# Attention-value products for two token tiles at once (256 columns) in two of six groups, with three wider transposed buffers and five staging buffers instead of seven

## The chip, the cores and the metric

One core of a Trainium2 chip runs the whole program. The metric is the device time of one execution in microseconds (us), the median over runs. The engines of the core run their own instruction streams in order: PE (TensorE: matmuls and transposes; PEld are its weight loads), DVE (VectorE), ACT (ScalarE), POOL (GpSimd) and SP, which here only starts DMA transfers.

## What is computed

```python
def _attn_ref(q, k, v):                      # 2 batches, 8 heads, 576 tokens, head size 64, fp32
    scores = scale * q @ k^T                 # per batch and head
    keep the 32 largest scores of each row, softmax over them
    return attn @ v

x = attention output as [1152 tokens, 512]
h = x @ w_in;  g = max(h, 0) + alpha * min(h, 0);  x = g @ w_out          # 512 -> 2048 -> 512
a = x @ w_a;   b = x @ w_b;                        out = (a * b) @ w_out2  # 512 -> 1536 -> 512
```

The weights arrive as 64-bit floats and are converted to fp32 on the chip.

## The kernel before, in words

**Token groups.** The 1152 tokens are cut into six groups (`M1`, line 46). A unit `('T', b, t)` is tile `t` of 128 tokens of batch `b`, `('L', b, 0)` the last 64 tokens of a batch. Groups 0, 1 and 5 hold one T tile, groups 2 and 4 two T tiles of one batch, group 3 two L units and a T tile. Attention walks the groups in order, in a group the four head pairs `hp`, and in a head pair the units. Each T unit gives two attention tiles, one for each head of the pair, each L unit one (lines 373 to 378): 72 attention tiles in all.

**One attention tile.** `front` (396) multiplies q with k into PSUM and ACT copies the 128x576 scores to `s`. `middle` (409) is the top-32 search on DVE (four MAX8, three MATCH_REPLACE8), the exponential on ACT, and the masked sum on DVE; POOL scales the rows (430). `back` (436) transposes the 576 columns in five pieces on PE (441, 443) and ACT copies them into a buffer `pt` of 5 x 128 columns (442, 444). `pt` has two buffers (`PB`, 41), one for each head of a pair. `back` of a tile is issued while DVE is in the next tile's search.

**The product with v.** When both heads of a unit are done, `av` (450) issues ten fp32 matmuls: for each of the five 128-row pieces one matmul for each head, with a 128x64 slice of `v` as the weights and `pt[:, c, :]` (128 columns) as the moving data. Head 0 writes the upper 64 partitions of the PSUM tile `o`, head 1 the lower 64. The profile records each fp32 matmul as two, so one call of `av` is 20 records and 20 weight loads, all at line 463. ACT (468) and DVE (469) then write `o` as two fp16 parts into `xT` of the group at the unit's columns (group 0 uses one ACT copy, line 471). `o` shares two PSUM buffers (tag "T") with the transposes of `back` and of `finish`. There are 40 calls of `av`: the 1st to 4th in time belong to group 0, the 5th to 8th to group 1, the next 8 to group 2, the next 12 to group 3, the next 8 to group 4, the last 4 to group 5.

**The two feed-forward stages.** For each group `moe1` (549) and `moe2` (636) run; `ORDER` (48) puts them in the order (1,0), (2,0), (1,1), (2,1), (1,2), (2,2), (1,3), (2,3), (1,4), (1,5), (2,4), (2,5), where the first number is the stage and the second the group. Matmuls into the hidden layers are at lines 530 and 534, those out of them at 542 and 545. The first chunk of `moe1`'s contraction over features is head pair 0, the last is head pair 3. The first stages use fp32 weights; later ones use weights split into two fp16 parts (`pair`, 239, on ACT and POOL), which for the last weight are kept in DRAM and fetched through three buffers `w2s` (`W2B`, 33).

**The staging ring.** Each of 68 weight blocks is loaded as 64-bit numbers into a staging buffer `raw` of 4 KB per partition (185) and read by ACT twice (190, 191) and by DVE once (192); POOL adds the parts (193). `RAWB` (53) is the number of such buffers, seven. Four tiles `v_raw` of `x_scale` (143) use the same ring; ACT squares them (141). The first 14 blocks are mixed with the first 8 attention tiles, then come the `v_raw` tiles, then 54 blocks, then the other attention tiles (line 52). When the last staging buffer is free, its space becomes that of the "late" pool (317), which holds `xT`, so that no group but group 0 can write `xT` earlier.

**Order.** The program is a single list of instructions with priorities; at build time each engine's order is fixed with the help of a simulated timeline (882), which also decides when a buffer is waited for. A different number of buffers or a different call can therefore change the order on every engine.

Of the kernel before, what the change touches and what calls it, by code (L numbers as in the profile page):

```python
# [8 lines left out]
F32 = mybir.dt.float32  # L9
# [7 lines left out]
AF = mybir.ActivationFunctionType  # L17
ALU = mybir.AluOpType

P = 128  # L20
B, H, S, D = 2, 8, 576, 64
# [16 lines left out]
OB = 2  # L38
EB = 3
WKB = 1  # L40
PB = 2
JB = 1
XB = 3
GB = 4
# [5 lines left out]
NATIVE = {(1, 0): (0, 0), (2, 0): (0, 0), (1, 1): (1, 0), (2, 1): (0, 0)}  # L50
STAGES = [(k, g if isinstance(g, tuple) else (g,)) + NATIVE.get((k, g), (1, 1)) for k, g in ORDER]
DVE = [('open', 0), ('mix', 14, 8), ('xs', 0), ('conv', 54), ('att', 80)]
RAWB = 7
FA = 4
QA = 1
VA = 0
# [24 lines left out]
def tile_topk_attention_moe(ctx: ExitStack, tc: tile.TileContext, qT, kT, vM, vL, wi, wo, al, wa, wb, w2, out):  # L81
    nc = tc.nc
    cp = ctx.enter_context(tc.tile_pool(name="cp", bufs=1))
    sp = ctx.enter_context(tc.tile_pool(name="sp", bufs=2))
# [4 lines left out]
    def psum(name, tag="H"):  # L89
        return pp.tile([P, 512], F32, tag=tag, name=name, bufs=2)  # L90
# [52 lines left out]
    def x_scale():  # L143
        for hp in range(4):
            v = early.tile([P, DM], I64, tag="raw", name="v_raw", bufs=RAWB).bitcast(F32)[:, 0:5 * P]
            v = v.rearrange("p (c n) -> p c n", c=5)
# [36 lines left out]
    def to_f32(dst, name, i):  # L183
        raw = early.tile([P, DM], I64, tag="raw", name="raw", bufs=RAWB)
        nc.sync.dma_start(raw, srcs[name][i])
        lo = raw.bitcast(U32).rearrange("p (n t) -> p n t", t=2)[:, :, 0]
        hi = raw.bitcast(I32).rearrange("p (n t) -> p n t", t=2)[:, :, 1]
        d = dst.bitcast(I32)
        r = early.tile([P, DM], I32, tag="rlo", name="rlo", bufs=RLOB)
        nc.scalar.activation(r.bitcast(I16).rearrange("p (n t) -> p n t", t=2)[:, :, 0], lo, AF.Copy, scale=2.0 ** -29)  # L190
        nc.scalar.activation(r.bitcast(BF16).rearrange("p (n t) -> p n t", t=2)[:, :, 1], hi.bitcast(F32), AF.Sign)
        nc.vector.tensor_scalar(d, hi, 3, None, op0=ALU.logical_shift_left)
        nc.gpsimd.tensor_tensor(out=d, in0=d, in1=r, op=ALU.add)
# [171 lines left out]
    tiles = []  # L365
    gsize = []
    for g, grp in enumerate(M1):
        cols_of = {}
        col = 0
        for kind, b, t in grp:  # L370
            cols_of[kind, b, t] = col
            col += P if kind == "T" else D
        for hp in range(4):
            for kind, b, t in grp:
                n = P if kind == "T" else D
                heads = [[2 * hp], [2 * hp + 1]] if kind == "T" else [[2 * hp, 2 * hp + 1]]
                for i, hs in enumerate(heads):
                    tiles.append(dict(g=g, b=b, t=t if kind == "T" else 4, hp=hp, hs=hs, n=n, col=cols_of[kind, b, t], last=i == len(heads) - 1))
        gsize.append(col)

    def fetch(tl):
# [53 lines left out]

    def back(tl):
        e = tl["e"]
        pt = sp.tile([P, 5, P], F32, tag="pt", name="pt", bufs=PB)
        t1, t2 = psum("t1", "T"), psum("t2", "T")
        for c in range(4):  # L440
            nc.tensor.transpose(t1[:, c * P:(c + 1) * P], e[:, c * P:(c + 1) * P], ident)  # L441
        nc.scalar.activation(pt[:, 0:4, :].rearrange("p c n -> p (c n)"), t1, AF.Copy)  # L442
        nc.tensor.transpose(t2[:, 0:P], e[:, S - P:S], ident)
        nc.scalar.activation(pt[:, 4, :], t2[:, 0:P], AF.Copy)
        tl["pt"] = pt

    def split_view(t):
        return t.rearrange("p c n -> p (c n)").bitcast(F16).rearrange("p (a c n) -> p a c n", a=2, c=4)

    def av(pair_):  # L450
        tl = pair_[-1]
        g, hp, n, col = tl["g"], tl["hp"], tl["n"], tl["col"]
        v = vcur[g, tl["b"], hp]
        if g not in xts:
            if split_in[g] or gsize[g] > P:
                xts[g] = late[0].tile([P, 4, 256], F32, tag="xT", name=f"xT{g}", bufs=XB)
            else:
                xts[g] = sp.tile([P, 4, P], F32, tag="xe", name=f"xe{g}", bufs=2)
        o = psum("o", "T")
        for c in range(5):  # L460
            for j in range(2):
                pt = pair_[j]["pt"] if n == P else tl["pt"]
                nc.tensor.matmul(o[j * D:(j + 1) * D, 0:P], v[:, c, j * D:(j + 1) * D], pt[:, c, :], start=c == 0, stop=c == 4)  # L463
        for r, c in [(slice(0, P), slice(0, P))] if n == P else [(slice(0, D), slice(0, D)), (slice(D, P), slice(D, P))]:
            if split_in[g]:
                x = split_view(xts[g])
                xh = x[r, 0, hp, col:col + n]
                nc.scalar.activation(xh, o[r, c], AF.Copy, scale=vsc[r, 0:1])
                nc.vector.scalar_tensor_tensor(x[r, 1, hp, col:col + n], o[r, c], vsc[r, 0:1], xh, op0=ALU.mult, op1=ALU.subtract)  # L469
            else:  # L470
                nc.scalar.activation(xts[g][r, hp, col:col + n], o[r, c], AF.Copy)

    def attention():
# [11 lines left out]
        for i, tl in enumerate(tiles):  # L485
            s = ready.pop(0)
            for k, _ in enumerate(middle(tl, s)):
                if k == 0 and i + FA < len(tiles):
                    fetch(tiles[i + FA])
                if k == 1 and i + VA < len(tiles):  # L490
                    fetch_v(tiles[i + VA])
                if k == KBACK and prev is not None:
                    back(prev)
                    pr.append(prev)
                    if prev["last"]:
                        av(pr)
                        pr = []
                    yield ("done", prev["g"])
                if k == KFRONT and i + QA < len(tiles):
                    ready.append(front(tiles[i + QA]))  # L500
                yield 1
            prev = tl
        back(prev)
        pr.append(prev)
        av(pr)
        yield ("done", prev["g"])

# [378 lines left out]
```

## Time and profile before

| what | value |
|---|---|
| median of three runs | 750.46 us (750.15 to 750.53) |
| the profiled execution, its own time | 752.66 us |
| its span, first to last instruction | 750.6 us |
| mean granted TensorE clock | 0.951 |
| instructions | 14910 |

The profiled execution is 2.2 us above the median, and 2.1 us of it lie outside the span. Busy times are sums over an engine's instructions; because matmul ends are modelled, a PE busy share of 100% says that PE never stood idle, not that it computed at its peak.

### The profile page before, as it was taken

Reading aid. Unit: us, or ns where it says so; the run is one execution under the profiler, and the core shown is the slowest. Engines: PE = TensorE matmul, PEld = TensorE weight load, DVE = VectorE, ACT = ScalarE, POOL = GpSimd, SP = SyncE. Lnnn points to the kernel's source line nnn. Section 1 sums busy time; section 2 is a strip of 40 time slices with the busy share of each in tenths; the row PEclk is TensorE's granted clock in tenths of the full one; section 3 lists DMA queues with packets and bytes.
Section 4 is the critical chain, followed back from the end, with each engine's and each line's share of the span. In section 5 each row is a group of like instructions: output and inputs, shape, how many; then the busy total and the mean of one; then the engine's idle time right before and its main releaser. Section 6 shows DMA issues by size and latency. Waiting matters only on the chain.

```text
span 750.6 us, 14910 instructions
## 1 busy us (share of the span) xinstructions
PE 653.1 (87%) x5162; PEld 491.0 (65%) x5162; DVE 600.7 (80%) x1478; ACT 476.8 (64%) x1011; POOL 394.2 (53%) x540
## 2 busy tenths in 40 slices
PE   2565677899979798989976999999899999999997
PEld 1354555587766586867745777776677777677775
DVE  3999999979799989899889968999899799222121
ACT  4869786977588677888887634555644455453222
POOL 5865888868465467878777522443233333131111
PEclk9997679899999898999998999999799999999999
DMA  6957977975420012330145632210122220001243
GB/s 198 332 142 257 312 255 257 320 275 195 136 71 24 11 59 70 94 90 22 55 129 177 185 90 67 77 28 12 30 66 65 73 74 1 2 1 43 72 127 99
DMA packets 60410, 86.16 MB, mean 115 GB/s; under 512 B 7984, under 2 KB 34608, under 8 KB 60336
## 3 DMA queue, kind: packets, MB, share of 16 engines
q1 hardware_dynamic: 59024, 82.87, 35.1%
q10 hardware_dynamic: 1312, 2.36, 0.9%
q8 instruction: 40, 0.66, 0.4%
q14 instruction: 34, 0.28, 0.1%
HBM read 76.55 MB, written 8.65 MB: 114 GB/s over the span
## 4 chain that ended last, share of the span: by engine, by line
PE 57%; DVE 21%; DMA 7%; ACT 7%; issue 4%; POOL 3%; SPq 1%; POOLq 0%; ACTq 0%; DVEq 0%
PE h L530 8%; PE y L542 7%; PE o L542 7%; PE ha L530 7%; PE hb L530 7%; PE o L463 5%; DVE wk L420 4%; DVE m L422 4%; DMA w2s<-w_st 3%; DVE e L426 3%; PE t L441 3%; PE ps L403 3%; PE ha L534 2%; PE hb L534 2%; PE o L545 2%
## 5 line engine op out<-in xcount | busy, mean ns | idle before, releaser
L422 DVE MAX8 m<-wk 128x8 f32<-128x576 f32 x216 | 162.9, 754 | 2.5
L521 POOL TENSOR_TENSOR gp<-gt,gp 128x256 f16<-128x256 f32 (+1 forms) x112 | 68.3, 611 | 153.9 <-ACT gp L520 143.8
L420 DVE MATCH_REPLACE8 wk<-m,wk 128x576 f32<-128x576 f32 x144 | 106.7, 741 | 0.0
L530 PE MATMUL h<-xT,wi_sb 128*128 128x256 f16 (+1 forms) x960 | 100.0, 253 | 2.3 <-DVE xT L469 1.3
L530 PEld LDWEIGHTS <-wi_sb 128*128 128x128 f16 x960 | 79.6, 99 | 22.9 <-issue 7.1
L430 POOL TENSOR_SCALAR e<-e,sm 128x576 f32<-128x576 f32 x72 | 55.1, 765 | 66.5 <-DVE sm L428 52.0
L542 PE MATMUL y<-wo_sb,gp 128*128 128x512 f16 x336 | 85.4, 380 | 1.7 <-ACT gp L520 1.7
L542 PEld LDWEIGHTS <-gp 128*128 128x128 f16 x588 | 54.7, 98 | 46.9 <-ACT gp L520 2.8
L520 ACT ACTIVATE gp<-gt 128x256 f16<-128x256 f32 (+1 forms) x112 | 43.2, 388 | 61.9 <-DVE gt L666 43.2
L426 DVE SCALAR_TENSOR_TENSOR e<-s,m,e 128x576 f32<-128x576 f32 x72 | 73.4, 1020 | 10.0 <-ACT e L416 7.7
L403 PE MATMUL ps<-ks,qh 128*128 128x288 f32 x160 | 49.4, 391 | 28.0 <-ACT s L406 15.2
L666 DVE SCALAR_TENSOR_TENSOR gt<-hb,wb_inv,r 128x256 f32<-128x256 f32 (+1 forms) x48 | 21.4, 446 | 61.6 <-PE hb L530 61.2
L463 PE MATMUL o<-pt,v 128*64 128x128 f32 x800 | 64.1, 298 | 6.3 <-ACT pt L442 3.8
L530 PE MATMUL ha<-xT,wa_sb 128*128 128x256 f16 (+1 forms) x576 | 66.0, 265 | 0.4 <-ACT xT L612 0.4
L414 DVE MAX8 m<-s 128x8 f32<-128x576 f32 x72 | 53.9, 748 | 15.2 <-ACT s L406 15.0
L542 PE MATMUL o<-w2s,gp 128*128 128x512 f16 x252 | 63.9, 379 | 1.8 <-DMA w2s<-w_pr 1.4
L463 PEld LDWEIGHTS o<-pt,v 128*64 128x64 f32 x800 | 49.3, 147 | 24.6 <-issue 7.8
L530 PE MATMUL hb<-xT,wb_sb 128*128 128x256 f16 (+1 forms) x576 | 65.2, 263 | 0.0
L416 ACT ACTIVATE e<-s,nb 128x576 f32<-128x576 f32 x72 | 55.7, 775 | 12.5 <-POOL nb L415 12.3
L530 PEld LDWEIGHTS <-wa_sb 128*128 128x128 f16 x576 | 51.7, 100 | 14.0 <-issue 2.1
L441 PE MATMUL t<-ident,e 128*128 128x128 f32 x288 | 50.5, 299 | 9.7 <-POOL e L430 4.4
L406 ACT ACTIVATE s<-ps 128x576 f32<-128x576 f32 x72 | 46.5, 645 | 17.9 <-DVE e L426 12.1
(191 smaller groups left out, 1455.0 us busy)
## 6 DMA issues: line engine op xcount, KB each, us to landing
w2s<-w_pr SPq DMA_DIRECT2D x48, 256.0 KB, 2.6
w2s<-w_st SPq DMA_DIRECT2D x36, 256.0 KB, 2.7
raw<-in_wi_dram SPq DMA_DIRECT2D x16, 512.0 KB, 5.8
raw<-in_wo_dram SPq DMA_DIRECT2D x16, 512.0 KB, 5.2
v<-in_vM_dram SPq DMA_DIRECT2D x28, 256.0 KB, 3.1
raw<-in_wa_dram SPq DMA_DIRECT2D x12, 512.0 KB, 4.5
raw<-in_wb_dram SPq DMA_DIRECT2D x12, 512.0 KB, 5.3
raw<-in_w_dram SPq DMA_DIRECT2D x12, 512.0 KB, 5.0
```

The lines of the kernel that those rows point to most:

```text
L403: nc.tensor.matmul(ps[:, f, 0:HALF], q[:, h % 2, :], ks[h][:, f * HALF:(f + 1) * HALF], start=i == 0, stop=i == len(mm) - 1)
L414: nc.vector.max(m8[:, 0:8], s)
L416: nc.scalar.activation(e, s, AF.Exp, bias=nb, scale=0.125)
L420: nc.vector.match_replace(out=wk, in_to_replace=m8[:, 8 * r - 8:8 * r], in_values=src, imm_value=NEG)
L422: nc.vector.max(m8[:, 8 * r:8 * r + 8], wk)
L426: nc.vector.scalar_tensor_tensor(e, s, m8[:, 31:32], e, op0=ALU.is_ge, op1=ALU.mult, accum_out=sm[:, 0:1])
L430: nc.gpsimd.tensor_scalar(e, e, sm[:, 1:2], 1.0, op0=ALU.mult, op1=ALU.mult)
L441: nc.tensor.transpose(t1[:, c * P:(c + 1) * P], e[:, c * P:(c + 1) * P], ident)
L463: nc.tensor.matmul(o[j * D:(j + 1) * D, 0:P], v[:, c, j * D:(j + 1) * D], pt[:, c, :], start=c == 0, stop=c == 4)
L521: nc.gpsimd.tensor_sub(l[:, 0:n], t[:, 0:n], h[:, 0:n])
L530: nc.tensor.matmul(dst[:, 0:n], w[a][:, c * P:(c + 1) * P], x[:, b, c, 0:n], start=k == 0, stop=k == 11)
L542: nc.tensor.matmul(dst, act[b][:, s], w[a], start=i == 0 and k == 0, stop=i == last and k == 2)
```

## The change

In groups 2 and 4 the two T units of a head pair become one unit of two slots. `back` writes each tile's transposed pieces into its 128 columns of a `pt` buffer that is now 5 x 256 columns wide in every group. `av` is called once for both slots, after the fourth attention tile instead of after the second and the fourth: ten matmuls with 256 columns instead of twice ten with 128, and then one ACT and one DVE instruction over 256 columns instead of two each over 128. The other groups keep 128 columns. `PB` goes from 2 to 3: `pt` takes 15 KB per partition instead of 5. `RAWB` goes from 7 to 5: the staging ring takes 20 KB per partition instead of 28.

```diff
-PB = 2
+PB = 3
-RAWB = 7
+RAWB = 5
...
+            units = []
             for kind, b, t in grp:
...
+                if units and len(units[-1]) < 2 and kind == "T" and units[-1][0][:2] == (kind, b):
+                    units[-1].append((kind, b, t))
+                else:
+                    units.append([(kind, b, t)])
+            for unit in units:
+                pts_of = {}
+                for slot, (kind, b, t) in enumerate(unit):
+                    n = P if kind == "T" else D
+                    heads = [[2 * hp], [2 * hp + 1]] if kind == "T" else [[2 * hp, 2 * hp + 1]]
+                    for i, hs in enumerate(heads):
+                        tiles.append(dict(g=g, b=b, t=t if kind == "T" else 4, hp=hp, hs=hs, n=n, col=cols_of[unit[0]], slot=slot,
+                                          wide=len(unit) * P, pts=pts_of, last=slot == len(unit) - 1 and i == len(heads) - 1))
...
     def back(tl):
...
-        pt = sp.tile([P, 5, P], F32, tag="pt", name="pt", bufs=PB)
+        j = tl["hs"][0] % 2
+        if tl["slot"] == 0:
+            tl["pts"][j] = sp.tile([P, 5, 2 * P], F32, tag="pt", name="pt", bufs=PB)
+        pt = tl["pts"][j][:, :, tl["slot"] * P:tl["slot"] * P + P]
...
     def av(pair_):
...
+        wd = tl["wide"]
         for c in range(5):
             for j in range(2):
-                pt = pair_[j]["pt"] if n == P else tl["pt"]
-                nc.tensor.matmul(o[j * D:(j + 1) * D, 0:P], v[:, c, j * D:(j + 1) * D], pt[:, c, :], start=c == 0, stop=c == 4)
-        for r, c in [(slice(0, P), slice(0, P))] if n == P else [(slice(0, D), slice(0, D)), (slice(D, P), slice(D, P))]:
+                pt = tl["pts"][j if n == P else 0]
+                nc.tensor.matmul(o[j * D:(j + 1) * D, 0:wd], v[:, c, j * D:(j + 1) * D], pt[:, c, 0:wd], start=c == 0, stop=c == 4)
+        if n == P:
+            n = wd
+        for r, c in [(slice(0, P), slice(0, wd))] if n > D else [(slice(0, D), slice(0, D)), (slice(D, P), slice(D, P))]:
```

## Rows read from the trace of the kernel before

**Rows 1.** The page's first part: busy time of each engine over the span, its share and its instructions.

```profile
PE 653.1 (87%) x5162; PEld 491.0 (65%) x5162; DVE 600.7 (80%) x1478; ACT 476.8 (64%) x1011; POOL 394.2 (53%) x540
```

**Rows 2.** The table by stretch: start and end in us, length, then busy us of PE, PEld, DVE, ACT and POOL (with instructions), granted clock, DMA share, GB/s. The stretches run from the first of the 54 blocks (61) to the opening of the late pool (192), on to the last call of group 2 (324), and then from the start of stage (2,2) (424) to that of stage (1,4) (598), to the end of attention (646) and to the end.

```profile
61.00:192.00 131.00, 103.81 (x705) 79.98 (x706) 122.36 (x310) 103.14 (x212) 103.73 (x109) 0.86 0.79 269
192.00:324.00 132.00, 118.11 (x901) 90.88 (x899) 121.21 (x325) 102.43 (x215) 82.12 (x107) 0.94 0.21 64
...
424.00:598.00 174.00, 170.47 (x1362) 127.92 (x1362) 155.56 (x371) 87.76 (x196) 56.08 (x100) 0.97 0.21 62
598.00:646.00 48.00, 48.00 (x393) 35.23 (x391) 37.96 (x89) 24.11 (x56) 16.20 (x27) 1.00 0.12 35
646.00:751.00 105.00, 99.47 (x977) 74.05 (x974) 22.52 (x62) 36.03 (x94) 20.64 (x41) 0.99 0.21 61
```

**Rows 3.** The chain of waits in order of time (start us, us on the chain, what): the fetches of the last split weight, the first matmuls of stage (2,2), and a call of `av` in group 4.

```profile
417.68 2.65 DMA w2s<-w_st
421.11 2.87 DMA w2s<-w_pr
424.02 1.46 PE o L542 x6
...
426.89 1.31 PE hb L530 x12
...
474.82 1.24 PE o L463 x20
```

**Rows 4.** The view of the tile `pt`: duration ns min/median/max, first and last start in us, forms; its weight loads.

```profile
L463 PEld LDWEIGHTS o<-pt,v x800: 132/137/232, 37.4 to 644.6; 128*64 128x64 f32 x160
```

**Rows 5.** PE's timeline (start us, us, engine, line, operation, count, idle time before it): calls of `av` in groups 2 (two) and 3, the last piece of the last call in group 4, and the first matmuls of stage (1,4).

```profile
297.95 2.40 PE L463 MATMUL o<-pt,v 128*64 128x128 f32 x20
...
324.17 1.31 PE L463 MATMUL o<-pt,v 128*64 128x128 f32 x20
...
415.51 1.09 PE L463 MATMUL o<-pt,v 128*64 128x128 f32 x16 [0.31 <-ACT pt L442]
...
585.83 0.43 PE L463 MATMUL o<-pt,v 128*64 128x128 f32 x2
...
597.63 0.71 PE L530 MATMUL h<-xT,wi_sb 128*128 128x256 f16 x5
```

**Rows 6.** Groups of ACT and DVE instructions by line and shape (count, busy us, mean ns of one, idle time before and its releaser): the reads of `o` at 128 columns, reads of other PSUM tiles at 256, and copies of 128x512 into a packed and into a strided tile.

```profile
L468 ACT ACTIVATE xT<-o,vsc 128x128 f16<-128x128 f32 x28 | 10.1, 364 | 13.3 <-PE o L463 13.2
L565 ACT ACTIVATE r<-h,pre_sig 128x256 f32<-128x256 f32 x48 | 22.5, 470 | 22.4 <-PE h L530 22.3
L469 DVE SCALAR_TENSOR_TENSOR xT<-o,vsc,xT 128x128 f16<-128x128 f32 x28 | 9.4, 339 | 2.3 <-ACT xT L468 2.2
L566 DVE SCALAR_TENSOR_TENSOR gt<-h,pre_alp,r 128x256 f32<-128x256 f32 x48 | 22.7, 474 | 7.7 <-ACT r L565 7.5
L619 ACT ACTIVATE xT<-tp 128x512 f32<-128x512 f32 x1 | 0.6, 597 | 0.0
L619 ACT ACTIVATE xe<-tp 128x512 f32<-128x512 f32 x1 | 0.6, 582 | 0.0
```

**Rows 7.** The timeline of DVE and PE after the last call of group 2.

```profile
326.27 2.76 DVE L426 SCALAR_TENSOR_TENSOR e<-s,m,e 128x576 f32<-128x576 f32 x1
...
329.69 0.34 DVE L469 SCALAR_TENSOR_TENSOR xT<-o,vsc,xT 128x128 f16<-128x128 f32 x1
...
331.11 0.61 PE L530 MATMUL h<-xT,wi_sb 128*128 128x256 f16 x4
```

**Rows 8.** Who waited for whom (us in total, times, longest): POOL on the last matmul of `av`, from 424 to 646 us.

```profile
POOL v L338 <- PE o L463: 8.6, 7, 2.9
```

**Rows 9.** The view of the tile `raw`: last blocks' loads and reads (first and last start), and the time from issue to landing of all its loads.

```profile
L185 SPq DMA_DIRECT2D raw<-in_w_dram x12: 327/328/358, 98.0 to 172.2; - x12
L192 DVE TENSOR_SCALAR wa_sb<-raw x12: 411/841/1495, 104.8 to 174.8; 128x512 int32<-128x512 int32 x12
L192 DVE TENSOR_SCALAR w2s<-raw x12: 411/488/1494, 109.1 to 191.5; 128x512 int32<-128x512 int32 x12
DMA to landing us min/median/max: 3.4/5.1/9.9
```

**Rows 10.** The timeline of SP, ACT and DVE where the 54 blocks begin: the ACT reads that free staging buffers, the first load of the 54, its DVE read, and ACT's first read of a `v_raw` tile.

```profile
60.17 0.75 ACT L191 ACTIVATE rlo<-raw 128x512 bf16<-128x512 f32 x1
60.95 0.34 SPq L185 DMA_DIRECT2D raw<-in_wi_dram  x1
62.66 0.76 ACT L191 ACTIVATE rlo<-raw 128x512 bf16<-128x512 f32 x1
64.39 1.39 DVE L192 TENSOR_SCALAR wi_sb<-raw 128x512 int32<-128x512 int32 x1 [0.17 <-DMA raw<-in_wi_dram]
64.47 0.73 ACT L141 ACTIVATE vsq<-v_raw 128x640 bf16<-128x640 f32 x1
```

**Rows 11.** SP's timeline where the third weight begins: three staging loads in a row.

```profile
92.08 0.52 SPq L185 DMA_DIRECT2D raw<-in_wa_dram  x1
...
96.12 0.33 SPq L185 DMA_DIRECT2D raw<-in_wb_dram  x1
98.04 0.33 SPq L185 DMA_DIRECT2D raw<-in_w_dram  x1
```

**Rows 12.** What SP's queue waited for (us in total, times, longest): staging loads on the ACT read that frees their buffer.

```profile
SPq L185 <- ACT rlo L191: 39.4, 29, 3.4
```

More of the change, by code (lines that the diff above doesn't have):

```diff
@@ L373, in tile_topk_attention_moe @@
         for hp in range(4):
+            units = []
             for kind, b, t in grp:
[L375 to L378, printed above, removed]
+                if units and len(units[-1]) < 2 and kind == "T" and units[-1][0][:2] == (kind, b):
[10 more added lines that the diff above has]
+                                          wide=len(unit) * P, pts=pts_of, last=slot == len(unit) - 1 and i == len(heads) - 1))
         gsize.append(col)
@@ L441, in back @@
             nc.tensor.transpose(t1[:, c * P:(c + 1) * P], e[:, c * P:(c + 1) * P], ident)
-        nc.scalar.activation(pt[:, 0:4, :].rearrange("p c n -> p (c n)"), t1, AF.Copy)
+        nc.scalar.activation(pt[:, 0:4, :], t1.rearrange("p (c n) -> p c n", c=4), AF.Copy)
         nc.tensor.transpose(t2[:, 0:P], e[:, S - P:S], ident)
         nc.scalar.activation(pt[:, 4, :], t2[:, 0:P], AF.Copy)
-        tl["pt"] = pt
     def split_view(t):
```

## The prediction, made before the changed kernel was run

> **What bounds the kernel now.** I read the busy shares first, then the table by stretch, then the chain of waits in time. The shares alone name PE: 653.1 of 750.6 us, with DVE at 600.7 [rows 1]. The stretches say where that is a limit. From 424 to 598 us PE is busy 170.47 of 174, then 48.00 of 48, then 99.47 of 105: 318 of the last 327 us, while DVE has 28 us to spare before attention ends at 646 and 82 of 105 after it [rows 2]. From there on the end is the sum of PE's work. Before it PE is idle: 27 us of the 131 from 61 to 192, 14 of the 132 to 324; there DVE, at 122.36 and 121.21, is nearer to its limit [rows 2]. PE's full stretch begins when the last split weight comes back from DRAM: the chain hops from fetch to fetch and enters stage (2,2) at 424 [rows 3]. So a PE microsecond saved behind 424 counts in full, one saved before it counts only if DVE or the conversion chain also moves.
>
> **The matmuls.** A call of av stands on the chain with 1.24 us for 20 records [rows 3]. How much of it is columns? A call of 20 records reads 1.31 us in the timeline, a piece of 16 reads 1.09 [rows 5], so a record costs (1.31 - 1.09) / 4 = 0.055 us. Twelve fp16 matmuls of 256 columns take 1.31 us, 0.109 each [rows 3], hence 0.055 for 128 columns. An fp32 record is two passes and the two heads fill two halves of the array at once; two passes over two halves is one pass, and 0.055 fits that. The 20 records are then 1.10 us of columns and 0.14 is the price of entering and leaving the half-array form. At 256 columns I expect 20 x 0.109 + 0.14 = 2.32 against 2 x 1.24 = 2.48: **0.16 us saved in each of 8 calls**. Four of them lie in group 4, between 474.82 [rows 3] and 585.83 [rows 5], where PE is full: -0.64. The four of group 2, 0.64 too, and more where the clock is low (one call there took 2.40 [rows 5]), lie where PE has 14 us idle; I count half, -0.3. The bounds of this term are 0 (columns alone, and all of group 2 hidden in idle time) and the rival below in which the loads set the pace.
>
> A rule speaks for more. The Trainium skill, "TensorE: Matmul & The Clock Gate", section "Back-to-back issue gap", gives a spacing per matmul of about 81 ns at 128 columns and 131 ns at 512, so four times the columns would cost 1.6 times; by it, as an estimate, a wide call would cost some 1.5 us and eight calls would save about 8 us. The trace speaks against it for this chain, where 256 columns cost twice the 0.055.
>
> **The reads of o.** In each of the eight pairs two ACT copies of 364 ns become one; the nearest row at 256 columns is 470 [rows 6]: -0.26 us, and I count nothing for it, since ACT is idle for a third of the span [rows 1]; the bound is group 2's four, -1.0. On DVE two of 339 become one near 474: -0.20 [rows 6]. For group 4 both are covered, since PE sets the time there; for group 2 DVE is 92% busy, so its 4 x 0.20 = 0.8 may count: bounds 0 and -0.8, I take -0.4. The shared PSUM pair "T" is asked for 8 times less; no row prices that alone, so it stays inside the bounds.
>
> **Writes to pt.** All 72 tiles now write a strided buffer. The one strided 128x512 copy took 597 ns, the packed one 582 [rows 6]: 72 x 0.015 = 1.1 us of ACT, spread over a span in which ACT is 64% busy [rows 1]. Bounds 0 and +1.1; I take 0, cover being ACT's idle time.
>
> **What is moved.** The first slot's product goes behind two more attention tiles. Its pt buffers are held longer; that is what the third buffer is for, and the next unit's second head needs the first buffer only two tiles after the wide call. The last wide call of a group ends about 1.1 us later than its narrow one did. In group 4 the last piece ran at 585.83 and stage (1,4) began at 597.63 [rows 5]: covered by 12 us. In group 2 stage (1,2) waits for it: av at 324.17 [rows 5], then DVE's read of o at 329.69, held by a 2.76 us DVE instruction in front of it, and the matmuls of the last chunk at 331.11 [rows 7]. The later end fits under that instruction; without it it would cost 1.1 us. POOL's clearing of the next v buffer waits for the end of av, 8.6 us in 7 waits behind 424 [rows 8]; each in group 4 may grow by 1.1 us, with the row scaling and the low-part subtraction queued behind it. POOL is busy 56.08 of 174 there [rows 2], and PE would have to run out of other matmuls before it shows: bounds 0 and +1.1 per group, I take 0. The number of DMAs is unchanged.
>
> **The ring of five.** This is the part that costs. Today each staging load leaves SP as ACT frees a buffer (read ends 60.17 + 0.75, load at 60.95 [rows 10]); SP spends 39.4 us waiting so [rows 12]. With five, a load waits for the buffer that is released two places later. At the start of the 54 blocks that is 62.66 + 0.76 = 63.42 instead of 60.95: +2.5 us, and with the load's 3.4 to 5.1 us [rows 9] DVE's read at 64.39, which even now waited for its data [rows 10], slips by as much; four of the five buffers are then v_raw tiles that ACT first reads at 64.47 [rows 10]. Later there is lead: the loads from 92.08 on were read from 104.8 on [rows 9, 11], 12.7 us; two places less (to 98.04 [rows 11]) leaves 6.8, still over the median landing of 5.1 but under the longest, 9.9 [rows 9]. What hides a slip is other DVE work (attention tiles are there to be pulled forward) and, at the end, that the last weight's load left at 172.2 and was read only at 191.5 [rows 9], so that its turn, not its data, set the end of conversion. Bounds: 0, and 2.5 us twice, +5. I take the end it is nearer to, given 19 us of lead at the end: **0**.
>
> **Sum.** -0.64 - 0.3 - 0.4 = -1.3 us. From the profiled execution's 752.66 that gives 751.3; the median of the runs shown is 2.2 lower, 750.46, so the forecast in its terms is **749.2 us**, inside the 0.2% (1.5 us) that a measurement of this kernel can tell from no change.
>
> **Rivals.**
> 1. **The ring takes PE's place as the early bound (slower).** Place: 61 to 192 us. If the conversion stream, rather than DVE's total work, sets when the late pool opens, the 2.5 us reach the first xT and the chain to 424, and a second slip near 100 to 170, where lead falls to 6.8, can add as much. It decides once a staging load lands after its turn on DVE. For it: SP is already queued behind ACT's reads [rows 12] and the first read already waits for its data [rows 10]. Against it: DVE is 93% busy there [rows 2] and the 19 us at the end. Price +1.5 to +6 after the gain: about 754.
> 2. **Weight loads set the pace (faster).** A load takes 137 ns [rows 4]; 20 of them on two halves are 1.37 us, close to the 1.24 of a call. If they and not the columns are the limit, a wide call costs little over 1.24, and eight save up to 9.9 us, of which group 4's 5.0 count in full: with the 0.4, about 745. Against it: 0.055 per record is exactly the fp16 column rate. The rule of the Trainium skill quoted above is this rival's. A changed order that fills PE's early idle time would end in the same place.
> 3. **Nothing arrives.** Group 4's 0.64 us and half the rest are eaten by the slips above: 750.5.
>
> **How the numbers follow.** The sum as worked out, -0.3 to -2.5, has a chance of 0.40, a little over half of it inside 0.2%; rival 3 has 0.12; rival 1 has 0.30; rival 2 has 0.06, and a better order 0.12. Faster by over 0.2% is 0.06 + 0.12 + 0.19 = 0.37; same 0.21 + 0.12 = 0.33; slower 0.30. The order on every engine is fixed anew at build time, and the 89 us in which PE is idle before 424 (424 less 653.1 - 317.94 [rows 1, 2]) is where that can move the time by some us either way. The range takes rival 2 down to 744 and rival 1 up to 756, and is signed on both sides because most of the chance is; the sum's own range is 747.9 to 750.2.
>
> **What would show it.** Right: eight calls at 256 columns near 2.3 us, 640 records at line 463 instead of 800, ACT's and DVE's reads of o near 470 ns, the start of stage (2,2) within 2 us of 424, PE full from there, and PE's busy time down by 1 to 1.5 us. Rival 1 shows as staging loads issued later, more DVE waiting for them near 64 us, and the last weight's last read after 191.5 us. Rival 2 shows as wide calls well under 2 us. The forecast is wrong if the start of stage (2,2) moves by more than 2 us, whatever the calls do.

## The result, and the profile after

The changed kernel takes **733.12 us** (median of four runs, 731.14 to 735.84; the kernel before 750.5 beside it): ratio 0.9766, interval 0.9738 to 0.9793. That is 17.4 us faster, where the forecast was 749.2 us and the range ended at 744. The profiled execution took 734.07 us, 732.3 of them its span, at a mean granted clock of 0.949. The ratio's interval is the one of the medians; all sums below compare the two profiled spans, 750.6 and 732.3 us, so 18.3 us are to be found.

Busy shares after, to be read against [rows 1]:

```profile
PE 644.0 (88%) x5002; PEld 477.6 (65%) x5002; DVE 594.0 (81%) x1470; ACT 471.9 (64%) x1003; POOL 391.9 (54%) x540
```

PE was busy 653.1 of 750.6 us and is busy 644.0 of 732.3: **9.1 us less busy time and 9.2 us less idle time** (97.5 to 88.3). The idle time goes with the ring; of the busy time, in these two executions, only about 2 us are less work and 7 us are less time lost at the low clock; the experiments show both. The table by stretch, at the times of [rows 2] (the stretch from 324 to 424 is one that the prediction left out; before it read as the first line):

```profile
324.00:424.00 100.00, 84.89 (x689) 62.56 (x689) 92.50 (x212) 82.57 (x167) 75.48 (x104) 0.97 0.34 105
```

```profile
61.00:192.00 131.00, 106.08 (x732) 82.20 (x733) 121.48 (x312) 104.77 (x219) 104.03 (x112) 0.84 0.82 270
192.00:324.00 132.00, 118.80 (x872) 85.95 (x871) 126.56 (x336) 106.52 (x222) 85.61 (x115) 0.96 0.27 76
324.00:424.00 100.00, 93.51 (x757) 69.44 (x756) 94.35 (x225) 82.93 (x170) 74.46 (x105) 0.97 0.34 105
424.00:598.00 174.00, 168.32 (x1286) 123.98 (x1282) 160.01 (x379) 88.86 (x196) 57.78 (x101) 1.00 0.22 64
646.00:733.00 87.00, 82.02 (x801) 62.14 (x798) 16.79 (x41) 25.95 (x67) 16.56 (x32) 0.98 0.26 74
```

Read the PE column: from 324 to 424 it rises from 84.89 to 93.51 us. The stages run ahead of their old times long before PE is full. PE's timeline, the first matmuls of stages (2,0), (1,1) and (2,2), before and then after, with (1,4) after, to be set beside the 597.63 of [rows 5] (stage (2,2) began at 404.55, not at the 424 of [rows 2] and [rows 3], where its matmuls out of the hidden layer begin):

```profile
154.46 0.71 PE L534 MATMUL ha<-xe,wa_sb 128*128 128x128 f32 x4
...
206.25 0.39 PE L530 MATMUL h<-xT,wi_sb 128*128 128x128 f16 x4
...
404.55 1.27 PE L530 MATMUL ha<-xT,wa_sb 128*128 128x256 f16 x5
```

```profile
149.41 0.77 PE L549 MATMUL ha<-xe,wa_sb 128*128 128x128 f32 x5
...
198.68 0.38 PE L545 MATMUL h<-xT,wi_sb 128*128 128x128 f16 x4
...
388.03 1.27 PE L545 MATMUL ha<-xT,wa_sb 128*128 128x256 f16 x5
...
579.36 0.83 PE L545 MATMUL h<-xT,wi_sb 128*128 128x256 f16 x6
```

5.1 us are won by the start of (2,0), 7.6 by (1,1), 16.5 by (2,2), 18.3 by (1,4). What such a gain looks like from close by: the longer idle times of PE in the 20 us in front of stage (2,2), before and then after (in brackets the idle time and what ended it).

```profile
387.24 0.60 PE L542 MATMUL y<-wo_sb,gp 128*128 128x512 f16 x2 [1.70 <-ACT gp L520]
...
394.34 0.53 PE L403 MATMUL ps<-ks,qh 128*128 128x288 f32 x2 [1.64 <-ACT s L406]
...
398.89 0.53 PE L403 MATMUL ps<-ks,qh 128*128 128x288 f32 x2 [1.61 <-POOL ks L332]
...
403.37 1.12 PE L441 MATMUL t<-ident,e 128*128 128x128 f32 x4 [2.67 <-ACT xT L612]
```

```profile
375.06 1.04 PE L557 MATMUL y<-wo_sb,gp 128*128 128x512 f16 x4 [0.81 <-POOL gp L536]
...
378.56 0.53 PE L413 MATMUL ps<-ks,qh 128*128 128x288 f32 x2 [1.38 <-ACT s L416]
...
385.41 1.01 PE L626 MATMUL tp<-ident,yb 128*128 128x128 f16 x8 [1.95 <-ACT xT L627]
```

There is no one long wait. PE runs its list in order, and each instruction that stands a little too early in it waits a microsecond or two for ACT, DVE or POOL: seven waits and 10.25 us before, six and 5.42 us after, the shorter ones not shown. Where an instruction stands is the build's choice, and that choice changed on every engine.

The calls that run in one piece did what was forecast. The chain of waits after (start us, us, what), against [rows 3]:

```profile
424.89 2.65 DMA w2s<-w_pr
427.58 1.46 PE o L557 x6
...
483.62 2.31 PE o L476 x20
```

Of the eight wide calls six stand in one piece and take about 2.3 us at full clock; two of group 2 are cut in pieces by other matmuls and take 2.9 and 3.0. Groups by line and shape after, against [rows 6]:

```profile
L455 ACT ACTIVATE pt<-t 128x512 f32<-128x512 f32 x72 | 43.0, 597 | 16.9 <-PE t L454 16.5
L476 PE MATMUL o<-pt,v 128*64 128x128 f32 x480 | 38.7, 301 | 1.0 <-ACT pt L455 1.0
L476 PE MATMUL o<-pt,v 128*64 128x256 f32 x160 | 22.2, 411 | 0.0
L483 ACT ACTIVATE xT<-o,vsc 128x256 f16<-128x256 f32 x8 | 3.8, 474 | 7.9 <-PE o L476 7.9
L484 DVE SCALAR_TENSOR_TENSOR xT<-o,vsc,xT 128x256 f16<-128x256 f32 x8 | 3.8, 473 | 0.1
```

And the tile `raw` after, against [rows 9]: loads leave later, the last DVE read starts 0.6 us later (192.1 against 191.5).

```profile
L185 SPq DMA_DIRECT2D raw<-in_w_dram x12: 327/328/559, 103.4 to 179.7; - x12
L192 DVE TENSOR_SCALAR w2s<-raw x12: 417/646/1422, 112.9 to 192.1; 128x512 int32<-128x512 int32 x12
```

### The profile page after: what moved, and what is told of

Same layout as the page of the kernel before. It is cut to its first block, busy times and chain, and to the rows that moved or that the text cites. A ratio compares the mean times of both kernels' runs of the same rounds, so it can differ in the third digit from the quotient of the medians.

```text
span 732.3 us, 14592 instructions
## 1 busy us (share of the span) xinstructions
PE 644.0 (88%) x5002; PEld 477.6 (65%) x5002; DVE 594.0 (81%) x1470; ACT 471.9 (64%) x1003; POOL 391.9 (54%) x540
## 5 line engine op out<-in xcount | busy, mean ns | idle before, releaser
L536 POOL TENSOR_TENSOR gp<-gt,gp 128x256 f16<-128x256 f32 (+1 forms) x112 | 70.6, 632 | 162.8 <-ACT gp L535 151.1
L535 ACT ACTIVATE gp<-gt 128x256 f16<-128x256 f32 (+1 forms) x112 | 43.4, 388 | 64.4 <-DVE gt L681 39.5
L557 PE MATMUL y<-wo_sb,gp 128*128 128x512 f16 x336 | 83.9, 380 | 0.8 <-POOL gp L536 0.8
L436 DVE SCALAR_TENSOR_TENSOR e<-s,m,e 128x576 f32<-128x576 f32 x72 | 67.0, 930 | 6.1 <-ACT e L426 3.9
L426 ACT ACTIVATE e<-s,nb 128x576 f32<-128x576 f32 x72 | 56.2, 783 | 17.7 <-POOL nb L425 17.4
L476 PE MATMUL o<-pt,v 128*64 128x128 f32 (+1 forms) x640 | 60.9, 329 | 1.0 <-ACT pt L455 1.0
L424 DVE MAX8 m<-s 128x8 f32<-128x576 f32 x72 | 53.9, 748 | 6.5 <-ACT s L416 6.3
L545 PEld LDWEIGHTS <-wb_sb 128*128 128x128 f16 x576 | 50.9, 99 | 7.9 <-issue 0.3
L190 ACT ACTIVATE rlo<-raw 128x512 int16<-128x512 uint32 x68 | 53.8, 791 | 2.5 <-DMA raw<-in_wo_dram 1.9
```

The costliest lines, as they stand in the source:

```text
L424: nc.vector.max(m8[:, 0:8], s)
L426: nc.scalar.activation(e, s, AF.Exp, bias=nb, scale=0.125)
L436: nc.vector.scalar_tensor_tensor(e, s, m8[:, 31:32], e, op0=ALU.is_ge, op1=ALU.mult, accum_out=sm[:, 0:1])
L476: nc.tensor.matmul(o[j * D:(j + 1) * D, 0:wd], v[:, c, j * D:(j + 1) * D], pt[:, c, 0:wd], start=c == 0, stop=c == 4)
L536: nc.gpsimd.tensor_sub(l[:, 0:n], t[:, 0:n], h[:, 0:n])
L545: nc.tensor.matmul(dst[:, 0:n], w[a][:, c * P:(c + 1) * P], x[:, b, c, 0:n], start=k == 0, stop=k == 11)
```

## The experiments

Three theories. **R**: five staging buffers make the conversions run better. **M**: the merged products save more than their own 0.16 us a call. **O**: neither; the build writes a new order on every engine and this one is a good draw. A first hint for O came from comparing the lists of instructions: with the ring of five alone, the traces have another instruction in 2387 of PE's 5162 places and in 1017 of DVE's 1478. The third `pt` buffer moves nothing, by the lists that the build writes: the kernel before with three, and the changed kernel with two, have on every engine the same order as with two and with three.

### One part at a time

e1 is the kernel before with five buffers; e2 the changed kernel with the ring of seven (and, for space, two `pt` buffers); e3 and e4 the changed kernel merging in group 2 or group 4 alone.

```diff
-RAWB = 7          # e1: in the kernel before
+RAWB = 5
-PB = 3            # e2: in the changed kernel
-RAWB = 5
+PB = 2
+RAWB = 7
...
-                if units and len(units[-1]) < 2 ...
+                if g == 2 and units and len(units[-1]) < 2 ...     # e3; e4: g == 4
```

> The kernel before with five staging buffers instead of seven and nothing else. Theory R (the shorter ring paces the conversions and lets attention run ahead): 733 to 738 us, with attention's 48th masked sum near 441 us as in the changed kernel. Theory M (merging the products of two token tiles is what pays): 749 to 753. Theory O (the gain comes from the order that the build fixes anew for every variant, with no sign of its own for either part): anywhere from 735 to 755.

> The changed kernel with seven staging buffers and two pt buffers, so that the merging of two token tiles is all that differs from before. Theory M: 731 to 737 us. Theory R: 748 to 750, the 1.3 us of the saved matmul time and no more. Theory O: anywhere from 735 to 755, not predictable from the other runs.

> The changed kernel (five staging buffers, three pt buffers) with the merging in group 2 only; group 4 goes back to two calls of 128 columns. Theory M: half the gain, 740 to 745 us; the saved matmul time of group 4 alone is 0.7 us, so if group 4's merging does no more than that, 733 to 735. Theory R: 733 to 735. Theory O: anywhere from 733 to 755.

> The changed kernel with the merging in group 4 only. Theory M: half the gain, 740 to 745 us. Theory R: 733 to 735. Theory O: anywhere from 733 to 755, and not the sum of the parts.

Measured: ring alone 742.46 us, ratio 0.9873 (0.9825 to 0.9921); merging alone 745.49, 0.9929 (0.9897 to 0.9961); group 2 alone 738.36, 0.9833 (0.9788 to 0.9878); group 4 alone 740.34, 0.9856 (0.9802 to 0.9909). Neither part is the whole; the two nearly add up, -1.3% and -0.7% to the change's -2.3%. Merging in one group alone gains less on top of the ring (0.4% in group 2, 0.2% in group 4) than merging in both (1.1%), but the intervals are half a per cent wide on each side: these two runs don't decide between M and R. What ring and merging take differs. Busy shares of e1, then of e2:

```profile
PE 651.8 (88%) x5162; PEld 489.2 (66%) x5162; DVE 597.6 (81%) x1478; ACT 475.5 (64%) x1011; POOL 391.8 (53%) x540
```

```profile
PE 643.0 (87%) x5002; PEld 478.6 (65%) x5002; DVE 601.7 (81%) x1470; ACT 473.9 (64%) x1003; POOL 394.7 (53%) x540
```

Of 740.9 us PE is idle 89.1 in e1; of 741.4 us it is idle 98.4 in e2. The ring took idle time (97.5 to 89.1) and left the busy time; merging took busy time (653.1 to 643.0) and left the idle time. How much of that busy time is work is split further down. O isn't excluded, since each kernel is one order.

### The same work in another order

The planner's charge for an attention item or its factor on TensorE's times is nudged; the instructions stay.

```diff
-T_ATT = 6.1       # e5: in the kernel before
+T_ATT = 6.2
-F_PE = 1.1        # e6: in the kernel before
+F_PE = 1.11
-RAWB = 7          # e7: in the kernel before
+RAWB = 6
```

> The kernel before with the same work, the same ring of seven and no merging; only the planner's charge for an attention item goes from 6.1 to 6.2, which lets other ready work stand elsewhere in the streams. If each part of the change has a gain of its own (the ring about -9 us, the merging about -6 us alone), nothing of either is here: within 3 us of the kernel before, 748 to 754, with the stall of DVE near 442 to 454 us about as long. If what counts is the order that the build writes (theory O), the time moves by as much as either part did, 5 us or more in either direction: 735 to 745 or 755 to 765.

> The kernel before with the same work; only the planner's factor on TensorE's estimated times goes from 1.10 to 1.11. As for the run with the other charge: 748 to 754 if ring and merging have gains of their own; 5 us or more away, in either direction, if the order alone does it. TensorE's busy sum should stay at 653 +- 2 us, so what moves is its idle time (97.5 us before).

> The kernel before with six staging buffers instead of seven, no merging. Five alone took 9 us off. If a shorter ring helps by what it does to the loads (theory R), six lies between: 743 to 750, about 746, and the early loads are delayed by less than with five. If the number only makes the build write another order (theory O), no rule ties six to five: anywhere from 738 to 758.

Measured: e5 751.6 us, ratio 1.0002 (0.9978 to 1.0026); e6 745.2, 0.9931 (0.9906 to 0.9956); e7 757.05, **1.0091** (1.0059 to 1.0124). With six buffers the kernel is 0.9% slower, with five 1.3% faster: not what R expects of a shorter ring. And e6 gains 0.7% with nothing changed but an order. Its gain isn't idle time. The table by stretch, before and then e6, from 155 us on:

```profile
155.00:424.00 269.00, 238.51 (x1878) 182.95 (x1877) 248.07 (x628) 211.88 (x442) 186.12 (x244) 0.96 0.32 98
424.00:751.00 327.00, 317.93 (x2726) 237.21 (x2725) 216.04 (x521) 147.90 (x345) 92.92 (x168) 0.98 0.20 58
```

```profile
155.00:424.00 269.00, 237.50 (x1911) 180.88 (x1910) 250.25 (x628) 211.43 (x443) 183.53 (x246) 0.98 0.32 97
424.00:745.00 321.00, 310.93 (x2670) 231.26 (x2667) 213.41 (x517) 144.00 (x335) 89.90 (x164) 0.99 0.20 59
```

The granted clock (last column but two) is higher in both stretches, and PE's sum falls from 653.1 to 644.4 with the same 5162 matmuls. To take that apart, add up from every PE record its busy time to the start of the next one, and halve it where the clock was at 1.2 GHz: work at full clock, and a surcharge. One thing has to be seen first. A trace's rows of the clock begin only with its first change, a rise, at 54 to 60 us in before, e1, e2, e5, e6 and e7 and at 36 to 42 in the others, and the table by stretch shows a clock of 1.00 before that; yet a call of `av` there takes 2.40 us instead of 1.31, so that time too was at the low clock. In the kernel before:

```profile
37.38 2.40 PE L463 MATMUL o<-pt,v 128*64 128x128 f32 x20 [0.47 <-ACT pt L442]
```

With it counted as low, before is 609.2 us of work and 43.9 of surcharge, e6 610.6 + 33.8: the gain is the surcharge. It doesn't look like one execution's luck: the granted clock of e6's ten executions is 0.961 to 0.971, that of the nineteen of the kernel before beside them 0.937 to 0.959.

### The changed kernel in other orders, and two narrow sets

e8 keeps the deferral, the buffers and the one evacuation per pair, but issues two sets of ten 128-column passes. e11 and e12 are the changed kernel with the two nudges of e5 and e6.

```diff
+        for w0 in range(0, wd, P):                                  # e8
...
-                nc.tensor.matmul(o[j * D:(j + 1) * D, 0:wd], ..., pt[:, c, 0:wd], ...)
+                    nc.tensor.matmul(o[j * D:(j + 1) * D, w0:w0 + P], ..., pt[:, c, w0:w0 + P], ...)
```

> The changed kernel, but each merged item issues two sets of ten 128-column passes instead of one set of ten 256-column passes; the deferral of the first tile, the double buffers, the one evacuation per pair and the ring of five stay. If the merging gains by the wide passes (theory M as TensorE time), what those saved is given back: busy of TensorE up by 1 to 3 us from 644.0 and the time at 734 to 737. If it gains by the deferral and by fewer evacuations, 732 to 734. If the order decides (theory O), the time may land anywhere from 733 to 745 and doesn't follow TensorE's busy sum.

> The changed kernel with the same work, buffers and merging; the planner's charge for an attention item goes from 6.1 to 6.2. If ring and merging have gains of their own: 730 to 736. If the 733 is largely a good draw among orders (theory O): 737 to 750. TensorE's busy sum stays at 644 +- 3 us in both cases.

> The changed kernel with the same work; the planner's factor on TensorE's times goes from 1.10 to 1.11 (in the kernel before that step alone took 6 us off). Gains of their own: 727 to 736. Order (theory O): anywhere from 730 to 750, with no rule that ties it to the step's effect on the kernel before. Together with the run with the other charge and the changed kernel itself it gives three orders of the merged work, against five of the unmerged (751, 752, 745, 742, 757): if merging has a part of its own, their mean lies 3 to 6 us under that of the five.

Measured: e8 742.67 us, 0.9892 (0.9845 to 0.9939); e11 734.39, 0.9777 (0.9731 to 0.9823); e12 737.27, 0.9841 (0.9801 to 0.9881). So 733 isn't a single lucky order. e8 loses 9.5 us to the changed kernel, more than any theory of wide passes gave: work at full clock rises from 607.0 to 610.3, and PE's idle time from 88.3 to 93.3. The products account for 1.8 us of the work (53.9 against 52.1 at full clock); the idle time is likely order again, which this run can't show. Its timeline says what the width itself is worth. Two narrow sets in a row, uncut, in group 4:

```profile
486.77 2.40 PE L477 MATMUL o<-pt,v 128*64 128x128 f32 x40
```

That is the time of a wide call (2.38 in the timeline, at the end of this text) and less than two separate narrow calls (1.31 each). So a clean call gains by standing next to the other, not by its 256 columns.

### The ring with the later order held

Here the build fixes the order by priorities and free buffers alone (`schedule_with_timeline_sim=False`). Then seven and five buffers differ only in the order of the conversions and of the attention tiles between them: on DVE no record after the 573rd of 1478, at some 302 us, stands elsewhere.

> The kernel before, same work, ring of seven, no merging, but the build fixes the order by priorities and free buffers alone, without the simulated timeline. It is the base for the next run, where a ring of five changes only the order of the conversions (DVE's instructions differ in the first third, in no later one), so that the ring can be weighed with the later order held. Its own time isn't foretold: 740 to 790.

> As the run before it, with five staging buffers instead of seven; after the ring is gone every engine's order is the same. If the ring has a gain of its own (theory R, -9 us as with the timeline's order), this is 5 to 10 us shorter than with seven. If the gain was the other order of the later work (theory O), it is within 3 us of the one with seven, or slower by up to 5 for the delayed loads.

Measured: 831.09 us with seven, ratio to the kernel before 1.1100 (1.1050 to 1.1151); 828.43 with five, 1.1047 (1.1007 to 1.1087). The intervals overlap. DVE's timeline, an instruction just behind the point from which the orders agree and the last masked sum, with seven, then with five:

```profile
302.61 0.74 DVE L420 MATCH_REPLACE8 wk<-m,wk 128x576 f32<-128x576 f32 x1
...
709.57 0.82 DVE L426 SCALAR_TENSOR_TENSOR e<-s,m,e 128x576 f32<-128x576 f32 x1
```

```profile
301.87 0.74 DVE L420 MATCH_REPLACE8 wk<-m,wk 128x576 f32<-128x576 f32 x1
...
707.72 0.82 DVE L426 SCALAR_TENSOR_TENSOR e<-s,m,e 128x576 f32<-128x576 f32 x1
```

0.7 us ahead where the orders meet, 1.9 at the end of attention. As O expects: within 3 us. The weak point is that this order is 80 us slower, so that a small help of the ring could be hidden in it.

### Three orders in each corner

e13 and e14 are the ring of five without merging, e15 and e16 merging with the ring of seven, each with `T_ATT = 6.2` and with `F_PE = 1.11`.

> Ring of five, no merging, the planner's charge for an attention item 6.2. With ring five and no merging there is one order so far (742.5). If the ring has a part of its own in the timeline's orders (theory R), all three orders with five lie near 742, 738 to 745, and so under the three with seven (751, 752, 745) by 5 or more in the mean. If order alone made the 742.5 (theory O), this one may be anywhere from 738 to 757, and the mean with five is within 3 us of the mean with seven.

> Ring of five, no merging, the planner's factor on TensorE's times 1.11. Same two expectations as the run before it: theory R 738 to 745; theory O 738 to 757.

> Merging alone (ring of seven), the planner's charge 6.2. One order of this so far: 745.5. If merging has a part of its own of 6 to 9 us (theory M), 740 to 746; if it has only the few tenths that the instructions' times say and the rest is order, 742 to 755.

> Merging alone (ring of seven), the planner's factor 1.11. Same two expectations: theory M 738 to 746; theory O 742 to 755. With this run there are three orders in each of four corners (ring seven or five, merged or not): if the differences of the corners' means are larger than the scatter inside a corner (so far 2 to 4 us), the two parts have effects of their own beside the order; if not, the 17 us of the change are a draw.

Measured: e13 739.31 us, 0.9857 (0.9831 to 0.9882); e14 743.84, 0.9915 (0.9883 to 0.9947); e15 743.86, 0.9916 (0.9888 to 0.9944); e16 744.69, 0.9933 (0.9908 to 0.9957). All four corners, each as base order, `T_ATT`, `F_PE` (idle is the span less PE's busy sum; work and surcharge as above):

| ring, products | ratios to before | PE idle, us | PE work at full clock, us | surcharge, us | calls of groups 2 and 4 at full clock, us |
|---|---|---|---|---|---|
| 7, single | 1, 1.0002, 0.9931 | 97.5, 96.5, 100.1 | 609.2, 609.4, 610.6 | 43.9, 45.8, 33.8 | 22.3, 21.8, 21.8 |
| 5, single | 0.9873, 0.9857, 0.9915 | 89.1, 89.1, 90.4 | 611.1, 612.2, 612.4 | 40.7, 36.6, 38.3 | 22.7, 22.8, 21.6 |
| 7, merged | 0.9929, 0.9916, 0.9933 | 98.4, 97.2, 94.0 | 607.2, 609.6, 608.7 | 35.8, 35.6, 39.5 | 19.1, 19.7, 20.1 |
| 5, merged | 0.9766, 0.9777, 0.9841 | 88.3, 87.5, 89.5 | 607.0, 609.0, 605.6 | 37.0, 30.7, 44.0 | 19.9, 20.3, 19.8 |

Read it by columns. **Five buffers take PE idle time**: 8.5 and 8.1 us, in time 1.0% and 1.3%. **Merging takes time**, 0.5% and 0.9%, 4 and 6.5 us, and its own calls take 2.3 us less in both rings. The rest of its gain isn't as clear: all PE work falls by 1.2 us in the mean with seven buffers, where the three orders with it and the three without overlap, and by 4.7 with five, where they don't. With seven buffers e6 is as fast without merging as the three orders with it. The surcharge is that of one execution each and scatters by 4 to 13 us inside a corner. The two orders that stand furthest from the base order of their corner, e6 and e12 at -0.7% and +0.75%, go with it: -10.1 and +7.0 us, though e12's profiled execution is the slowest of its four. And the three orders of a corner are not three draws for the ring: of DVE's first 400 records, up to some 184 us, `T_ATT` changes no place, `F_PE` 58 or 70, the ring 274. The stages that the ring could touch are nearly the same order three times.

### Which wait is it?

In all six kernels with seven buffers PE waits 6.6 to 7.5 us between 78 and 155 us for the diagonal sum `junk` of a block's squares (line 210); in the nine with five 1.3 to 1.9; in e7, with six, 8.4. The view of waits, of before, e1 and e7 (us, times, longest):

```profile
PE gram L205 <- DVE junk L210: 6.7, 6, 2.1
```

```profile
PE gram L205 <- DVE junk L210: 1.9, 4, 0.6
```

```profile
PE gram L205 <- DVE junk L210: 8.4, 7, 2.1
```

It fits all of them, so I tried to take that wait away without touching the ring: two calls of `square` share a PSUM tile, e17 in the kernel before, e18 in the changed one.

```diff
-        gram = psum("gram", "Y")
+        if gbank["n"] % 2 == 0:
+            gbank["t"] = psum("gram", "Y")
+        gram = gbank["t"][:, gbank["n"] % 2 * 256:gbank["n"] % 2 * 256 + 256]; gbank["n"] += 1
```

> The kernel before (ring of seven, no merging), but two successive calls of square share one PSUM tile, one half each, so that the matmuls of the second call don't wait for DVE's diagonal sum (junk) of the first. In all six kernels with seven buffers PE waits 6.6 to 7.5 us for junk between 78 and 155 us, in all with five 1.3 to 1.9. If that stall is what the ring of five removes, the wait falls under 3 us here, stage (2,0) starts at 147 to 151 us instead of 154.5, and the time is 742 to 747. If the stall only goes along with something else that five buffers do, the wait falls but stage (2,0) starts at 153 to 155 and the time stays at 748 to 753.

> The changed kernel with the same shared PSUM tile. Its wait for junk is only 1.9 us, so if that wait is the mechanism there is little left to take: 730 to 735. If the halves help in another way as well (the bank is asked for half as often), up to 5 us less: 727 to 730. A new order may cost or give 3 us either way, as with the other orders of the changed kernel (733, 734, 737).

Measured: e17 **741.22 us**, 0.9896 (0.9840 to 0.9952); e18 739.97, 0.9865 (0.9818 to 0.9912). The wait in e17:

```profile
PE gram L209 <- DVE junk L214: 6.0, 5, 1.9
```

The edit didn't remove the wait, yet stage (2,0) starts at 149.54 us, (1,1) at 198.36, PE's idle time is 89.6 and the time is that of the ring of five. So the wait for `junk` doesn't by itself set the start of (2,0), and my explanation falls: it went along with the ring in sixteen traces and caused nothing that I can show. What e17 does show is that the 8 us come with seven buffers too. The edit changes the order and also how often the PSUM tile is asked for, so it doesn't tell which of the two did it. e18 shows that the same edit costs the changed kernel about 7 us; the wait for `junk` rises there from 1.9 to 5.7 us and (2,0) starts 3.1 us later. No other version's median is under that of the changed kernel.

Where the idle time goes is plainer. From the first matmul of stage (1,1) to that of (2,2), in before, e1 and e17 (columns as in [rows 2]):

```profile
206.25:404.55 198.30, 171.53 (x1324) 128.47 (x1321) 185.34 (x446) 160.08 (x327) 138.06 (x187) 0.95 0.24 70
```

```profile
197.80:392.60 194.80, 176.61 (x1363) 131.46 (x1361) 185.79 (x453) 161.33 (x334) 135.03 (x188) 0.95 0.26 73
```

```profile
198.40:391.80 193.40, 174.15 (x1353) 126.99 (x1352) 185.60 (x438) 158.91 (x329) 137.73 (x187) 0.97 0.24 70
```

PE idles 26.8, 18.2 and 19.3 us there; in all seven kernels with seven or six buffers it is 24.7 to 29.2, in the nine with five and in e17 and e18 17.3 to 21.3 (e9 and e10, with their other order, left aside). One thing in the order goes along with it in all eighteen: between the first matmul of (2,0) and that of (1,1) PE has three calls of `av` in the first seven and two in the other eleven, so that (1,1) begins a call, some score matmuls and some transposes sooner. That is a candidate like the one before, not yet a cause: no run moves it alone.

## Why the prediction was wrong, step by step

- **Where PE sets the end.** Right: PE is busy 168.32 of 174 us from 424 and 82.02 of the last 87. The step also said that before 424 a saving counts only if something else moves; it did: 16.5 of the 18.3 us are there by the first matmul of stage (2,2).
- **The calls.** 2.32 us forecast, 2.31 measured for a call in one piece; 256 columns cost twice 128 here, as [rows 3] and [rows 5] said, and the estimate of 1.5 us from the Trainium skill's "TensorE: Matmul & The Clock Gate", "Back-to-back issue gap", isn't borne out. The 0.14 us for entering and leaving the half-array form fits e8, where two narrow sets in a row are as short as a wide call. But the **term was mis-sized**: 0.94 us against 2.3 in the calls of groups 2 and 4. I had priced both single calls at the clean 1.24, while in group 2 the timeline of the kernel before shows six of eight cut in pieces, at 1.4 to 1.6 us of full clock each, such as

```profile
275.63 1.31 PE L463 MATMUL o<-pt,v 128*64 128x128 f32 x18
...
278.22 0.43 PE L463 MATMUL o<-pt,v 128*64 128x128 f32 x2
```

  Merging gains 4 to 6.5 us in time. What it gains beyond its calls isn't traced: PE's work outside them falls by 2.4 us with five buffers and rises by 1.1 with seven. The forecast had no term for it.
- **Reads of o, writes to pt.** Right in size: 474 and 473 ns against 470 and 474; 597 against 592 for the copy.
- **What is moved.** The deferral cost nothing that shows; POOL's wait for the last matmul of `av` from 424 to 646 us is 7.2 us instead of 8.6. But the third buffer is inert: the step that explained what it is for was wrong.
- **The ring.** This is **the step that failed**: "Bounds: 0, and 2.5 us twice, +5." The late loads came as worked out (last load at 179.7 us instead of 172.2, DVE waiting 6.7 us for first-weight blocks instead of 5.7), and the end of the conversions stayed, as forecast. What was missing is a gain: I closed the bounds at nothing without a reason that excludes one, and the ring took 8 us of PE's idle time off, 1.0 to 1.3% of the time. I had priced the ring as a resource in a fixed order. It acts, as far as the runs show, as an input to the order: five -1.3%, six +0.9%, seven with a shared PSUM tile -1.0%, five against seven with the later order held -2.7 us of 831, inside the noise.
- **The chances.** The prediction named 89 us of idle time before 424 as "where that can move the time by some us either way" and gave "a better order" 0.12, with the time of rival 2. Rival 1 was seen in its signs and had no price at the end. The range's lower end of 744 came from rival 2 alone and was too near. The sum's own range, -0.3 to -2.5, isn't what its bounds add up to either: the gains alone come to 1.3 + 1.0 + 0.8 = 3.1 us.
- **The mark.** "The forecast is wrong if the start of stage (2,2) moves by more than 2 us": the matmul I had taken for it, the first one out of the hidden layer, moved from 424.02 to 427.58, later, while the stage's first matmul came 16.5 us earlier. It gave the right verdict by luck: that matmul waits for a fetch (2.65 us in the chain), and the work in front of it had moved the other way.

What stays open is which instructions have to stand where to give the 8 us; the call of `av` in front of (1,1) is the candidate, and no run isolates it.

## What to carry to other kernels

Where the build fixes the order anew, a change of a buffer count or a call has two prices, that of its work and that of a new order; the second went from nothing (e5) over -5 us (e6) to +7 (e7, with its ring of six) here, more than all the instructions' own terms, so the range must take it in on both sides. Tell the two apart by splitting PE's span into work at full clock, surcharge for the low clock and idle time, and by running the old and the new work in several orders made by a harmless nudge; and check in which stretch the nudge moves anything, or three orders are one, and from when on the trace has the clock. A wait that goes along with a gain in every trace is still only a candidate until it is taken away.

## What the runs showed of the hardware

The granted clock moved more between orders of the same work than I had expected: the surcharge for time at 1.2 GHz is 33.8 us in e6 against 43.9 before, and 44.0 in e12 against 37.0 after, one execution each. One wide call that ran into such a stretch took 4.07 us instead of 2.38. PE's timeline after, two calls of group 2, and the stretches around the first (granted clock third from the end): PE had been busy 8.08 of the 10 us to 286, and the clock then fell to 1.2 GHz for most of the next 4.

```profile
285.73 4.07 PE L476 MATMUL o<-pt,v 128*64 128x256 f32 x20
...
315.21 2.38 PE L476 MATMUL o<-pt,v 128*64 128x256 f32 x20
```

```profile
276.00:286.00 10.00, 8.08 (x56) 6.17 (x56) 9.35 (x31) 9.55 (x21) 6.39 (x15) 1.00 0.35 97
286.00:290.00 4.00, 4.00 (x22) 2.09 (x18) 4.00 (x17) 1.00 (x3) 2.88 (x2) 0.57 0.29 80
```
